# Sliding-window attention and a token MLP on one core: four stages in sequence, or one list-scheduled program

## The chip, the core and the metric

The kernel runs on one core of one Trainium2 chip. A core has five engines with queues of their own: TensorE (PE, matmuls, results only to PSUM), VectorE (DVE), ScalarE (ACT, activation functions), GpSimd (POOL) and SyncE (SP, which here only starts DMAs). Each engine works through its own instructions in the order in which the program gives them, and waits on semaphores for the others. PSUM is 8 banks of 128 x 512 float32. The metric is the device time of one execution in microseconds (us): 398.37 us, the median of three runs (398.35 to 398.4).

## The reference, cut to what matters

```python
def _A_ref(x, wqkv, wo):                      # x 1 x 2048 x 512, H = 32 heads of 16, window W = 256
    qkv = (x @ wqkv).reshape(B, S, 3, H, Dh).transpose(2, 0, 3, 1, 4)
    scores = jnp.einsum("bhqd,bhkd->bhqk", q, k) * (Dh ** -0.5)
    mask = (idx[:, None] - idx[None, :] >= 0) & (idx[:, None] - idx[None, :] < W)
    p = _softmax(jnp.where(mask, scores, -1e9))
    o = jnp.einsum("bhqk,bhkd->bhqd", p, v)
    return o.transpose(0, 2, 1, 3).reshape(B, S, D) @ wo
def _B_ref(x, w1, b1, w2, b2):                # mixes the 2048 tokens through F = 1376
    h = _layernorm(x)
    u = _gelu(jnp.einsum("bsd,sf->bdf", h, w1) + b1)
    return (jnp.einsum("bdf,fs->bds", u, w2) + b2).transpose(0, 2, 1)
g = _sigmoid((A_x * gate_w).sum(-1, keepdims=True))
return g * _A_ref(A_x, A_wqkv, A_wo) + (1 - g) * _B_ref(B_x...)
```

The kernel uses A_x for both branches, as the reference does. All tensors are bfloat16.

## The kernel before

Tokens are cut into 16 blocks of 128. The program is four stages, one after the other.

First the LayerNorm (L112 to L124: h_sb) and the gate (L126 to L136), from all of x (Xs, one load of 2 MB). x transposed (XT) comes from four transposing DMAs (L57). Then the first MLP matmul (L143 to L150): 11 chunks of F, each a chain of 16 matmuls of 128 x 512 into one PSUM bank, then GELU by hand on ACT and DVE (L153 to L161) into ug_sb. Third the projections (L192 to L213): Q twice, once with a copy of its weights in which the odd heads are zero (wqa) and once with the even ones zero (wqb), so that one 32-row operand (Qcomb) holds two heads side by side; K and V once; then the second MLP matmul (L215 to L225), 16 chains of 11, evacuated by ACT into b_sb.

Last the attention. A list of 180 steps (L243 to L248) runs over query block qb, the two or three key blocks kb that its window touches, and four groups gi of eight heads. emit_S does four score matmuls (L265: 32 rows by 256 columns, each for two heads, on two of the four 32-row groups of the array) into a two-bank PSUM tile Sp, one exp of 128 x 1024 on ACT (L273) into Et, and where the block is cut by the window a mask, on DVE (L275, diagonal) or POOL (L277, the far edge). Two steps later emit_PV does eight matmuls with Et as the loaded operand and 17 columns of V (16 and a column of ones, L301) into Op; after every second step DVE adds Op into osum in SBUF (L314, L316). When a query block is complete, emit_tailA normalises (L324, L326), transposes on PE (L333) and copies (L335); six steps later emit_tailB does the output projection (L342), the gated sum (L347, L349) and the store (L353). Sp has two buffers (ps_s), Et five (esb). The step list and the code order set the order on every engine.

Of the kernel before, what the change touches and what calls it, by code (L numbers as in the profile page):

```python
# [7 lines left out]
FP32 = mybir.dt.float32  # L9
# [4 lines left out]

@with_exitstack
def kernel(
# [21 lines left out]
    NQB = S // P  # L38
    NFC = (F + P - 1) // P
    EPS = 1e-5  # L40

# [3 lines left out]
    const = ctx.enter_context(tc.tile_pool(name="const", bufs=1))  # L45
    persist = ctx.enter_context(tc.tile_pool(name="persist", bufs=1))
    ugpool = ctx.enter_context(tc.tile_pool(name="ugpool", bufs=1))
    wts = ctx.enter_context(tc.tile_pool(name="wts", bufs=1))
    bphu = tc.alloc_tile_pool(name="bphu", bufs=1)

    Xs = persist.tile([P, NQB, D], BF16, name="Xs")
    nc.sync.dma_start(Xs[:], X.rearrange("(t p) d -> p t d", p=P))
    w1_sb = bphu.tile([P, NQB, F], BF16, name="w1_sb")
    nc.sync.dma_start(w1_sb[:], B_w1.rearrange("(t p) f -> p t f", p=P))
    XT = persist.tile([P, 4, S], BF16, name="XT")
    for ck in range(4):
# [12 lines left out]
    nc.gpsimd.dma_start(gw[:], gate_w.partition_broadcast(P))

    b1tmp = const.tile([P, NFC], BF16, name="b1tmp")
    b2tmp = const.tile([P, NQB], BF16, name="b2tmp")
    nc.gpsimd.memset(b1tmp[:], 0.0)
    with nc.allow_non_contiguous_dma(reason="tiny strided bias loads"):
        nc.gpsimd.dma_start(b1tmp[:, 0:NFC - 1], B_b1[0:(NFC - 1) * P].rearrange("(t p) -> p t", p=P))
        nc.gpsimd.dma_start(b1tmp[:F - (NFC - 1) * P, NFC - 1:NFC],
                            B_b1[(NFC - 1) * P:F].rearrange("(p o) -> p o", o=1))
        nc.gpsimd.dma_start(b2tmp[:], B_b2[:].rearrange("(t p) -> p t", p=P))

    ident = const.tile([P, P], BF16, name="ident")  # L80
# [156 lines left out]
    def e_col(kk, rl, par):  # L237
        return rl * 512 + kk * 256 + par * 128
# [164 lines left out]
```

## Time and profile before

| | us |
|---|---|
| median of three runs | 398.37 |
| span of the profiled execution, first to last instruction | 396.5 |
| MLP 1, projections, MLP 2 on PE | 32.8 to 170 |
| attention, 180 steps | 170.7 to 396.5 |
| PE busy / ACT busy / DVE busy / POOL busy | 340.3 / 229.1 / 203.4 / 81.2 |

No separate time is given for the profiled execution; its span is 1.9 us under the median, and that is taken as what lies around the span. To read the profile: a busy PE is not PE at its best, since matmuls overlap and their ends are modelled, so pitches (start to start) are used for PE; PEclk is the granted TensorE clock, 1.00 for 2.4 GHz and 0.50 for 1.2 GHz.

### The profile page before, as it was taken

How to read it: one execution, taken by the hardware profiler on the slowest of the kernel's cores; microseconds unless marked ns; L12 is line 12 of the kernel's file. 1: busy time of each engine (PE TensorE's matmuls, PEld its weight loads, DVE VectorE, ACT ScalarE, POOL GpSimd, SP SyncE). 2: the span in 40 equal slices, each digit the busy share in tenths (PEclk: the TensorE clock that was granted, in tenths of full speed). 3: DMA queues.
4: the chain of work that ended last, by engine and by line, in shares of the span. 5: the costliest groups of instructions: out<-in, count | busy, mean ns of one | idle time of the engine just before them, and what ended most of it. 6: DMA issues, size and time to landing. Idle time of an engine off the chain costs nothing.

```text
span 396.5 us, 6929 instructions
## 1 busy us (share of the span) xinstructions
PE 340.3 (86%) x2896; PEld 151.7 (38%) x2896; DVE 203.4 (51%) x410; ACT 229.1 (58%) x284; POOL 81.2 (20%) x80
## 2 busy tenths in 40 slices
PE   0006999899999999979999999999999999999982
PEld 0002444444444444433444444444344444444431
DVE  0199977743443100046556555545645645655653
ACT  1033433344333223277778778878877877977870
POOL 8300000020000000002143144044034124214300
PEclk9999999999999999985555555555555555555555
DMA  8999200096000000000000000000000000000000
GB/s 208 335 398 236 41 2 1 0 346 224 1 2 0 2 0 0 2 0 15 15 2 14 15 2 14 15 13 3 16 15 2 15 13 2 15 15 2 16 13 13
DMA packets 17423, 20.24 MB, mean 51 GB/s; under 512 B 8816, under 2 KB 13424, under 8 KB 17392
## 3 DMA queue, kind: packets, MB, share of 16 engines
q1 hardware_dynamic: 16160, 17.57, 13.7%
q10 hardware_dynamic: 1056, 2.10, 2.0%
q8 instruction: 22, 0.36, 0.4%
q0 software_dynamic: 176, 0.14, 0.3%
q14 instruction: 9, 0.07, 0.1%
HBM read 15.60 MB, written 2.10 MB: 45 GB/s over the span
## 4 chain that ended last, share of the span: by engine, by line
PE 46%; ACT 22%; DVE 13%; POOL 9%; DMA 4%; issue 4%; ACTq 0%; POOLq 0%
ACT Et L273 20%; PE Sp L265 10%; PE ps_proj L197 10%; PE ps_proj L219 10%; POOL Et L277 9%; PE aps L342 8%; PE Op L301 5%; DMA Xs<-in_A_x_dram 4%; PE ps_proj L208 3%; DVE stats L114 2%; DVE ug_sb L161 2%; DVE t L158 2%; DVE t L155 2%; ACT sg L160 2%; DVE h_sb L120 1%
## 5 line engine op out<-in xcount | busy, mean ns | idle before, releaser
L273 ACT ACTIVATE Et<-Sp 128x1024 bf16<-128x1024 f32 x180 | 173.3, 1028 | 42.1 <-PE Sp L265 42.0
L265 PE MATMUL Sp<-Qcomb,KT 32*128 32x256 bf16 x720 | 118.5, 393 | 8.7 <-ACT Et L273 7.9
L277 POOL TENSOR_SCALAR_AFFINE_SELECT Et<-Et 128x1024 bf16<-128x1024 bf16 x56 | 66.5, 1220 | 229.5 <-ACT Et L273 229.5
L301 PEld LDWEIGHTS <-Et 128*128 128x128 bf16 x1440 | 55.8, 106 | 89.5 <-DVE Et L275 38.8
L301 PE MATMUL Op<-VA,Et 128*128 128x17 bf16 x1440 | 69.8, 178 | 5.3 <-DVE Et L275 1.9
L148 PE MATMUL ups<-h_sb,w_sb 128*128 128x512 bf16 (+1 forms) x176 | 40.9, 397 | 33.3 <-DMA w_sb<-in_B_w_dram 32.8
L275 DVE TENSOR_TENSOR Et<-Et,Mge 128x1024 bf16<-128x1024 bf16 x64 | 42.8, 688 | 47.5 <-ACT Et L273 45.8
L316 DVE TENSOR_TENSOR osum<-Op,osum 128x272 f32<-128x272 f32 x58 | 25.6, 442 | 29.9 <-PE Op L301 29.9
L148 PEld LDWEIGHTS <-w_sb 128*128 128x128 bf16 (+1 forms) x176 | 18.2, 104 | 55.5 <-DMA w_sb<-in_B_w_dram 32.8
L219 PE MATMUL ps_proj<-ug_sb,w_sb 128*128 128x512 bf16 (+1 forms) x176 | 38.2, 379 | 0.0
L342 PE MATMUL aps<-wo_sb,OnT 128*128 128x512 bf16 x64 | 34.9, 610 | 0.5 <-DVE OnT L335 0.5
L265 PEld LDWEIGHTS <-KT 32*128 32x128 bf16 x720 | 26.9, 103 | 20.8 <-issue 16.6
L314 DVE COPY osum<-Op 128x272 f32<-128x272 f32 x32 | 14.1, 441 | 33.1 <-PE Op L301 32.0
L223 ACT ACTIVATE b_sb<-ps_proj,b2col 128x512 bf16<-128x512 f32 x16 | 11.0, 687 | 28.0 <-PE ps_proj L219 28.0
L219 PEld LDWEIGHTS <-w_sb 128*128 128x128 bf16 (+1 forms) x176 | 17.2, 98 | 20.9
L118 ACT ACTIVATE rstd<-mv,eps_col 128x1 f32<-128x1 f32 x16 | 4.6, 294 | 26.9 <-DVE mv L116 26.9
L183 ACT ACTIVATE Qcomb<-ps_proj 128x512 bf16<-128x512 f32 x16 | 11.8, 744 | 14.1 <-PE ps_proj L197 13.3
L185 DVE CAST Qcomb<-ps_proj 128x512 bf16<-128x512 f32 x16 | 11.6, 731 | 14.4 <-PE ps_proj L197 14.3
L160 ACT ACTIVATE sg<-t 128x512 f32<-128x512 f32 (+1 forms) x11 | 6.9, 630 | 20.5 <-DVE t L158 20.5
L197 PE MATMUL ps_proj<-XT,wqa 128*128 128x512 bf16 x64 | 14.1, 379 | 2.1 <-ACT uf L153 1.5
L347 DVE TENSOR_TENSOR diff<-aps,b_sb 128x512 f32<-128x512 f32 x16 | 11.1, 692 | 7.9 <-PE aps L342 7.9
L170 POOL MEMSET VA<- 128x512 bf16 x1 | 2.3, 2297 | 61.9 <-DVE ug_sb L161 61.9
(53 smaller groups left out, 231.4 us busy)
## 6 DMA issues: line engine op xcount, KB each, us to landing
w_sb<-in_B_w_dram SPq DMA_DIRECT2D x1, 5504.0 KB, 31.4
w_sb<-in_B_w_dram SPq DMA_DIRECT2D x1, 5120.0 KB, 17.1
Xs<-in_A_x_dram SPq DMA_DIRECT2D x1, 2048.0 KB, 17.7
out_dram<-outt SPq DMA_DIRECT2D x16, 128.0 KB, 1.7
wqkv_sb<-in_A_wqkv_dram ACTq DMA_DIRECT2D x1, 1536.0 KB, 13.5
wo_sb<-in_A_wo_dram ACTq DMA_DIRECT2D x1, 512.0 KB, 16.0
w_sb<-in_B_w_dram SPq DMA_DIRECT2D x1, 384.0 KB, 17.6
gw<-in_gate_w_dram POOLq DMA_DIRECT2D x1, 128.0 KB, 6.9
```

The costliest lines, as they stand in the source:

```text
L148: nc.tensor.matmul(ups[:fsz, :], lhsT=w1_sb[:, st, f0:f0 + fsz], rhs=h_sb[:, st, :], start=(st == 0), stop=(st == NQB - 1),)
L160: nc.scalar.activation(sg[:fsz, :], t1[:fsz, :], ACT.Tanh, scale=0.7978845608028654)
L197: nc.tensor.matmul(ps[:, :], lhsT=lhsT, rhs=XT[:, ck, sc * 512:(sc + 1) * 512], start=(ck == 0), stop=(ck == 3),)
L219: nc.tensor.matmul(yps[:, :], lhsT=w2_sb[:fsz, fc, st * P:(st + 1) * P], rhs=ug_sb[:fsz, fc, :], start=(fc == 0), stop=(fc == NFC - 1),)
L265: nc.tensor.matmul(Sp[:, col:col + 256], lhsT=KT[32 * r2:32 * r2 + 32, k, kb * P:(kb + 1) * P], rhs=rhs, start=True, stop=True, tile_posit ...
L273: nc.scalar.activation(out=Et[:], in_=Sp[:], func=ACT.Exp, scale=SCALE)
L275: nc.vector.tensor_tensor(out=Et[:], in0=Et[:], in1=Mge[:], op=ALU.mult)
L277: nc.gpsimd.affine_select(out=Et[:], in_=Et[:], pattern=[[0, 8], [-1, 128]], compare_op=ALU.is_gt, fill=0.0, base=0, channel_multiplier=1,)
L301: nc.tensor.matmul(Op[:, hl * DV:(hl + 1) * DV], lhsT=Et[:, col:col + 128], rhs=VA[:, kb, h, :], start=True, stop=True,)
L314: nc.vector.tensor_copy(out=dst, in_=Op[:, 0:16 * DV])
L316: nc.vector.tensor_tensor(out=dst, in0=Op[:, 0:16 * DV], in1=dst, op=ALU.add)
L342: nc.tensor.matmul(aps[:, :], lhsT=OnT[:, c2, :], rhs=wo_sb[:, c2, :], start=(c2 == 0), stop=(c2 == 3),)
```

## The change

The whole computation becomes a list of tasks (class Task: engines with a cost each, an emitting function, predecessors, a priority, buffers taken and used), and a planner (arrange) orders them once, when the program is built: it repeatedly takes the task that can start earliest by its costs, within a patience of 0.2 for the urgent ones by priority, gives it a buffer of a ring, and appends it. The instructions are then emitted in that order and stay in it on each engine.

- Attention goes by units of one query block, one half of the heads (hf, 16 heads) and one key block: 90 units. A unit is eight score matmuls on all four row groups into two Sp buffers (ring sp, three of two banks), two exps of 128 x 1024 into one Et of 128 x 2048 (ring et, five), one mask on 2048 columns, and 16 PV matmuls. The two or three key blocks of a group sum in one PSUM bank, so the adds of L316 and osum go; reciprocal and scaling read PSUM.
- Every other matmul result goes through ring gp, two banks: the projections, both MLP matmuls (chain, cut in pieces of two matmuls that other tasks can come between), PV, transposes, output projection, gate.
- Q is projected once; two evacuations multiply it by a 0/1 column (par) into QZ, one with the odd and one with the even heads zero. wqa and wqb go.
- x is loaded in four quarters, and XT comes from 64 PE transposes, evacuated by DVE. The gate's dot product goes to PE (64 matmuls of one column).
- The rstd is a power on POOL, and the tanh, exp and copies share one activation table. w1 and w2 share one buffer (wb), so w2's loads wait for the last MLP 1 matmul.
- Eight matmuls on zeros stand at the start of PE (warm). MLP 2 of a block is evacuated with gate and bias folded in (c1, c2), and one DVE instruction forms the output.

```diff
+def arrange(tasks, patience):
...
+            first = min(s for s, _ in found)
+            pick = min(
+                ((t.prio, s, i) for i, (s, t) in enumerate(found) if s <= first + (patience if t.prio < 10 else 0.0)),
+            )
+            start, t = found[pick[2]]
+            if best is None or (start, t.prio) < best[:2]:
+                best = (start, t.prio, e, t)
...
+    sp = ring("sp", 3, [P, 1024], FP32, "psum")
+    gp = ring("gp", 2, [P, 512], FP32, "psum")
+    et = ring("et", 5, [P, 2048], BF16, "sb")
...
-            nc.scalar.activation(rstd[:], mv[:, 1:2], ACT.Sqrt, bias=eps_col[:], scale=1.0)
+            nc.gpsimd.tensor_tensor(out=r, in0=r, in1=half[:], op=ALU.pow)
...
+    def chain(name, mms, deps, prio, piece=2):
+
+        b = gp.use()
...
+                    nc.tensor.matmul(buf(b)[:rows, :], lhsT=lhsT, rhs=rhs, start=(j == 0), stop=(j == n - 1))
...
+                for p in range(2):
+                    q.append(copy_out(
+                        f"qc{k}_{i}{p}", lambda k=k, p=p: QZ[:, i % NQ, p, k, :], lambda b=b: buf(b)[:],
+                        [t, k4] + free_q.get((k, i - NQ), []), 4, b, 0.53, scale=par[:, p:p + 1],
+                    ))
...
+    groups = [(qb, hf) for hf in range(2) for qb in range(4)]
+    groups += [(qb, hf) for qb in range(4, NT) for hf in range(2)]
...
-        for (kk, rl) in ((0, 0), (0, 1), (1, 0), (1, 1)):
+                for kk in range(2):
+                    k = 2 * hf + kk
+                    for r in range(4):
+                        nc.tensor.matmul(
+                            buf(b2[r // 2])[:, (r % 2) * 512 + kk * 256:(r % 2) * 512 + kk * 256 + 256],
...
+                            start=True, stop=True, tile_position=(32 * r, 0),
...
-                        lhsT=Et[:, col:col + 128],
-                        rhs=VA[:, kb, h, :],
-                        start=True, stop=True,
+                                buf(o)[:, hl * DV:(hl + 1) * DV], lhsT=buf(e)[:, col:col + 128], rhs=VA[:, kb, head, :],
+                                start=(first and hl == 0), stop=final, skip_group_check=True,
...
-                nc.vector.tensor_tensor(out=dst, in0=Op[:, 0:16 * DV], in1=dst, op=ALU.add)
...
+        dw2.append(add(f"w2_{i}", {"SP": 0.1}, emit, m1, 0.1 * i, lat=2.2 + 4.5 * (i + 1)))
...
+            lambda bp=bp, b=b, qb=qb: nc.scalar.activation(buf(bp)[:], buf(b)[:], ACT.Identity, bias=c2[:, qb:qb + 1], scale=c1[:, qb:qb + 1]),
...
+    plan = arrange(tasks, 0.2)
+    with tc.manual_schedule():
+        for t in plan:
+            t.emit()
```

What this does to the order shows at three places. **ACT in the attention.** Before, all 180 exps (L273) stand in one row behind everything else that ACT does:

```order
L183 ACTIVATE Qcomb<-ps_proj 128x512 x16
L183 ACTIVATE KT<-ps_proj 128x512 x8
L183 ACTIVATE VA<-ps_proj 128x32x16 x8
L223 ACTIVATE b_sb<-ps_proj,b2col 128x512 x16
L273 ACTIVATE Et<-Sp 128x1024 x180
```

Now (L474 is the exp, L637 the evacuation of an MLP 2 block into bp), around query block 8:

```order
L637 ACTIVATE bp_111<-gp_92,c_87,c_86 128x512
L474 ACTIVATE et_96<-sp_90 128x1024
L474 ACTIVATE et_96<-sp_88 128x1024
L474 ACTIVATE et_97<-sp_89 128x1024
L637 ACTIVATE bp_112<-gp_91,c_87,c_86 128x512
L474 ACTIVATE et_97<-sp_90 128x1024
L474 ACTIVATE et_93<-sp_88 128x1024
```

The evacuations stand between exps: the first exp comes after four evacuations instead of 102 activations of other kinds, and 65 other activations stand between the first exp and the last.

**PE in a late query block.** Before, PE alternates between four scores (L265) and eight PV matmuls (L301); only the output projection (L342) has 512 columns:

```order
L301 LDWEIGHTS Et
L301 MATMUL Op<-VA,Et 128x17
L265 LDWEIGHTS KT
L265 MATMUL Sp<-Qcomb,KT 128x256
L265 LDWEIGHTS KT
L265 MATMUL Sp<-Qcomb,KT 128x256
L265 LDWEIGHTS KT
L265 MATMUL Sp<-Qcomb,KT 128x256
L265 LDWEIGHTS KT
L265 MATMUL Sp<-Qcomb,KT 128x256
L342 LDWEIGHTS OnT
L342 MATMUL aps<-wo_sb,OnT 128x512
```

Now scores (L457) are followed by MLP 2 matmuls (L356, from ug and wb), here after the last unit's scores:

```order
L457 LDWEIGHTS KT
L457 MATMUL sp_90<-QZ,KT 128x256
L457 LDWEIGHTS KT
L457 MATMUL sp_90<-QZ,KT 128x256
L356 LDWEIGHTS wb
L356 MATMUL gp_92<-ug,wb 128x512
L356 LDWEIGHTS wb
L356 MATMUL gp_92<-ug,wb 128x512
L356 LDWEIGHTS wb
L356 MATMUL gp_92<-ug,wb 128x512
```

Between the first and the last score matmul PE now has 517 matmuls of 512 columns; before it had 60 there, all of the output projection.

**PE at the end.** Before, four output projection matmuls (L342) end the program:

```order
L333 LDWEIGHTS onrm
L333 MATMUL OnTp<-ident,onrm 128x128
L342 LDWEIGHTS OnT
L342 MATMUL aps<-wo_sb,OnT 128x512
L342 LDWEIGHTS OnT
L342 MATMUL aps<-wo_sb,OnT 128x512
```

Now the last MLP 2 chain (from ug and wb) and the last output projection (from wo and xo) do:

```order
L356 LDWEIGHTS wb
L356 MATMUL gp_92<-ug,wb 128x512
L356 LDWEIGHTS xo
L356 MATMUL gp_91<-wo,xo 128x512
L356 LDWEIGHTS xo
L356 MATMUL gp_91<-wo,xo 128x512
```

Behind the last score matmul stand 75 matmuls of 512 columns, 48 of PV and 4 transposes; before there were 24 of PV, 4 transposes and 4 of 512 columns.

## Rows read from the trace of the kernel before

**Rows 1.** The page: engine totals; then 40 slices, tenths busy and tenths of clock.
```profile
PE 340.3 (86%) x2896; PEld 151.7 (38%) x2896; DVE 203.4 (51%) x410; ACT 229.1 (58%) x284; POOL 81.2 (20%) x80
...
PE   0006999899999999979999999999999999999982
...
PEclk9999999999999999985555555555555555555555
```
**Rows 2.** The page: chain of work that ended last, shares of the span by engine.
```profile
PE 46%; ACT 22%; DVE 13%; POOL 9%; DMA 4%; issue 4%; ACTq 0%; POOLq 0%
```
**Rows 3.** Stretches: length; busy PE, PEld, DVE, ACT, POOL (x instructions); clock, DMA, GB/s.
```profile
79.90:118.00 38.10, 38.06 (x177) 17.28 (x177) 15.68 (x22) 15.78 (x23) 1.57 (x1) 1.00 0.40 149
132.00:170.00 38.00, 37.95 (x176) 17.03 (x175) 0.63 (x1) 10.32 (x16) 0.00 (x0) 1.00 0.00 1
171.00:175.00 4.00, 2.08 (x40) 1.01 (x33) 2.28 (x4) 3.78 (x5) 0.00 (x0) 0.96 0.00 0
175.00:385.00 210.00, 199.82 (x2224) 88.42 (x2223) 120.43 (x223) 168.50 (x175) 66.50 (x56) 0.50 0.03 11
```
**Rows 4.** Timeline of PE, high clock: start, length, line, operation, count, idle before.
```profile
170.73 0.41 PE L265 MATMUL Sp<-Qcomb,KT 32*128 32x256 bf16 x8 [0.78 <-ACT b_sb L223]
...
173.08 0.36 PE L301 MATMUL Op<-VA,Et 128*128 128x17 bf16 x8 [0.39 <-DVE Et L275]
173.37 0.40 PE L265 MATMUL Sp<-Qcomb,KT 32*128 32x256 bf16 x4
```
**Rows 5.** The same timeline of PE at the low clock.
```profile
176.98 0.61 PE L265 MATMUL Sp<-Qcomb,KT 32*128 32x256 bf16 x4
177.52 0.39 PE L301 MATMUL Op<-VA,Et 128*128 128x17 bf16 x8
177.84 0.61 PE L333 MATMUL OnTp<-ident,onrm 128*128 128x128 bf16 x4
178.38 0.61 PE L265 MATMUL Sp<-Qcomb,KT 32*128 32x256 bf16 x4
...
180.45 1.44 PE L342 MATMUL aps<-wo_sb,OnT 128*128 128x512 bf16 x3
181.82 0.61 PE L265 MATMUL Sp<-Qcomb,KT 32*128 32x256 bf16 x5
```
**Rows 6.** Timeline of ACT: exps that follow one another without a wait.
```profile
308.03 4.69 ACT L273 ACTIVATE Et<-Sp 128x1024 bf16<-128x1024 f32 x5 [1.12 <-PE Sp L265]
```
**Rows 7.** Groups by line and shape: busy us, mean ns | idle before, releaser.
```profile
L273 ACT ACTIVATE Et<-Sp 128x1024 bf16<-128x1024 f32 x180 | 173.3, 1028 | 42.1 <-PE Sp L265 42.0
...
L277 POOL TENSOR_SCALAR_AFFINE_SELECT Et<-Et 128x1024 bf16<-128x1024 bf16 x56 | 66.5, 1220 | 229.5 <-ACT Et L273 229.5
...
L183 ACT ACTIVATE Qcomb<-ps_proj 128x512 bf16<-128x512 f32 x16 | 11.8, 744 | 14.1 <-PE ps_proj L197 13.3 <-DVE ug_sb L161 0.8
...
L223 ACT ACTIVATE b_sb<-ps_proj,b2col 128x512 bf16<-128x512 f32 x16 | 11.0, 687 | 28.0 <-PE ps_proj L219 28.0
...
L153 ACT ACTIVATE uf<-ups,b1col 128x512 f32<-128x512 f32 x10 | 6.7, 673 | 0.2 <-DVE ug_sb L161 0.2
L160 ACT ACTIVATE sg<-t 128x512 f32<-128x512 f32 x10 | 6.3, 630 | 18.5 <-DVE t L158 18.5
...
L183 ACT ACTIVATE KT<-ps_proj 128x512 bf16<-128x512 f32 x8 | 4.8, 597 | 8.9 <-PE ps_proj L197 8.9
```
**Rows 8.** DMA issues: size and us from issue to landing.
```profile
w_sb<-in_B_w_dram SPq DMA_DIRECT2D x1, 5120.0 KB, 17.1
Xs<-in_A_x_dram SPq DMA_DIRECT2D x1, 2048.0 KB, 17.7
...
wqkv_sb<-in_A_wqkv_dram ACTq DMA_DIRECT2D x1, 1536.0 KB, 13.5
```
**Rows 9.** MLP 1 matmuls: count, shortest, median and longest ns, first and last start.
```profile
L148 PE MATMUL ups<-h_sb,w_sb x176: 376/379/634, 32.8 to 73.8; 128*128 128x512 bf16 x160, 128*96 128x512 bf16 x16
```
**Rows 10.** Timeline of the end: the last issue of a store.
```profile
393.46 0.33 SPq L353 DMA_DIRECT2D out_dram<-outt  x1
```

More of the change, by code (lines that the diff above doesn't have):

```diff
@@ L12, with __init__, use @@
 ALU = mybir.AluOpType
+class Buf:
+    def __init__(self, ring):
+        self.ring = ring
+        self.index = None
+        self.users = 0
+        self.end = 0.0
+class Ring:
+    def __init__(self, name, tiles):
+        self.name = name
+        self.tiles = tiles
+        self.avail = [0.0] * len(tiles)
+    def use(self):
+        return Buf(self)
+class Task:
+    def __init__(self, name, engines, emit, deps=(), prio=50.0, lat=None, takes=(), uses=(), at=0.0):
+        self.name = name
+        self.engines = dict(engines)
+        self.emit = emit
+        self.deps = [d for d in deps if d is not None]
+        self.prio = prio
+        self.lat = lat
+        self.takes = list(takes)
+        self.uses = list(uses)
+        for b in self.takes + self.uses:
+            b.users += 1
+        self.at = at
+        self.done = None
+        self.left = 0
+        self.next = []
+        self.ready = at
@@ new lines @@
+    KT = sb.tile([P, NK, 4, SB], BF16, name="KT")
+    QZ = sb.tile([P, NQ, 2, 4, SB], BF16, name="QZ")
+    VA = sb.tile([P, NT, H, DV], BF16, name="VA")
+    eps = sb.tile([P, 4], FP32, name="eps")
+    half = sb.tile([P, 4], FP32, name="half")
+    zeros = sb.tile([P, D], BF16, name="zeros")
+    ident = sb.tile([P, P], BF16, name="ident")
+    mask = sb.tile([P, P], BF16, name="mask")
+    par = sb.tile([P, 2], FP32, name="par")
+    gwc = sb.tile([P, 4], BF16, name="gwc")
+    b1t = sb.tile([P, NFC], BF16, name="b1t")
@@ new lines, in masks, with parity @@
+    def masks():
+        nc.gpsimd.memset(b1t[:], 0.0)
+        nc.gpsimd.memset(mask[:], 1.0)
+        nc.gpsimd.affine_select(
+            out=mask[:], in_=mask[:], pattern=[[1, P]], compare_op=ALU.is_ge, fill=0.0, base=0,
+            channel_multiplier=-1,
+        )
+    k2 = add("masks", {"POOL": 0.8}, masks, prio=1)
+    k3 = add("smalls", {"POOL": 4.0}, small_loads, [k2], prio=2, lat=6.0)
+    def parity():
+        v = ident[:].rearrange("p (r two d) -> p two r d", two=2, d=DH)
+        for i in range(2):
+            nc.vector.tensor_reduce(out=par[:, i:i + 1], in_=v[:, i], op=ALU.add, axis=mybir.AxisListType.XY)
@@ new lines, with biases @@
+    k4 = add("parity", {"DVE": 0.4}, parity, [k1], prio=0.5)
+    k5 = add("ones", {"POOL": 2.3}, lambda: nc.gpsimd.memset(VA[:, :, :, DH:DV], 1.0), prio=3)
+    def biases():
+        nc.vector.tensor_copy(b1c[:], b1t[:])
+        nc.vector.tensor_copy(b2c[:], b2t[:])
+    k6 = add("biases", {"DVE": 0.35}, biases, [k3], prio=30)
+    wu = gp.use()
+    warm = add(
+        "warm", {"PE": 3.4},
+        lambda: [nc.tensor.matmul(buf(wu)[:], lhsT=zeros[:, 0:P], rhs=zeros[:], start=True, stop=True) for _ in range(8)],
+        [k0], prio=0, takes=[wu],
+    )
```

707 lines of the change are left out of this document (428 added, 279 removed).

## Prediction

> **What bounds the kernel now.** First the page. PE is busy for 86% of the span, ACT for 58%, DVE for 51% [rows 1], and in the slices one sees that this is a mean over two programs: after the first loads PE is full all the way, but the TensorE clock is whole in the left half and half in the right. The chain that ended last gives PE 46% and ACT 22% [rows 2]. So the share of each engine has to be read by stage, and the stretches do that [rows 3]. In the projections PE is busy 38.06 of 38.10 us at clock 1.00, in MLP 2 37.95 of 38.00 us for 176 matmuls, a pitch of 38.0 / 176 = 0.216 us; ACT works 15.8 and 10.3 us there. These stages, from 32.8 to 170 us, have one limit, PE, and ACT's exps wait behind them. From 175 to 385 us PE is busy 199.8 of 210 us and ACT 168.5 of 210, and the clock is 0.50, which is 1.2 GHz. It fell some 5 us after the last 512-column matmul: from 171 to 175 us, with PE busy 2.08 of 4.00 us, it still averages 0.96. In the attention, then, PE at half clock is the limit and ACT is close behind: 180 exps need 173.3 us by their busy time [rows 7].
>
> The two halves use different engines, and nothing in the data forbids doing them together: MLP 1, MLP 2 and attention depend on each other only in the final sum. That is the room: 137 us of PE alone in front of 226 us of ACT and PE.
>
> **The change part by part: ACT.** An exp costs 4.69 / 5 = 0.938 us where five follow one another [rows 6]; 180 of them 168.8 us. Between the first and the last exp stand 65 others: 15 evacuations at 0.597, 16 that multiply by a column at 0.597 to 0.744 (I take 0.67), 11 bias adds at 0.673, 11 tanh at 0.630, 11 of MLP 2 at 0.687 [rows 7] and the gate's one of 0.2: 9.0 + 10.7 + 7.4 + 6.9 + 7.6 + 0.2 = 41.8 us. An exp alone takes 1.028 us against a pitch of 0.938, so neighbours overlap by 0.09, and 65 x 0.09 = 5.9 may come off: 205 to 211 us, and I take 207.
>
> **PE between first and last score.** At the high clock, dense matmuls: 517 x 0.216 = 111.7. Scores: a row shows eight of them, on all four row groups, within 0.41 us [rows 4], so a unit's eight cost at most 0.41; I take 0.40. PV: eight take 0.29 us from their start to the start of the next scores at the high clock [rows 4], 0.32 at the low one [rows 5]; sixteen 0.58. So 90 x 0.40 + 87 x 0.58 = 86.5. Transposes: four take 0.54 us at the low clock [rows 5], 0.135 each, and no more than that at the high one; 84 x 0.10 = 8.4. The gate's 64 columns go at the PV pitch of 0.036: 2.3. Sum 208.9. Removed with no cost left: 64 of the 128 Q matmuls (13.8 us at 0.216), and DVE's adds of PV.
>
> So ACT (207) and PE (209) are level over the same stretch, where before the same work stood at 137 + 214 us. Two engines that are both full and feed each other in a fixed order do not reach their sums. The row to size that by is the attention before: PE's needs per query block there are 12 x (0.54 + 0.32) + 0.54 + 4 x 0.43 = 12.6 us by pitch [rows 5], against 14.4 us that a block took (210 us for about 14.6 blocks), so 13% went into waits. Now there are three score buffers for two and room for ten exps for five, and I allow 6%: 12 us. Its ends are 0 and 13%, 27 us.
>
> **Start.** Before, all of wqkv (1.5 MB) landed after 13.5 us [rows 8]. The first score now needs two thirds of it: 9.0, from an issue at about 0.8: 9.8 us. A quarter of x is a quarter of 17.7 us, 4.4, and its transposes run before the weights are there. The bounds are 8 us (x quarter, 16 transposes and a copy alone set it) and 14.3 (the second load on the queue shares equally). Then four chains, 16 matmuls, at 0.216 or 0.432: after an idle stretch the first matmuls of MLP 1 took up to 634 ns against a median of 379 [rows 9], so PE begins low in spite of the eight on zeros; I take the middle, 5.2. An evacuation of 0.7 more: first score at 16, range 12 to 22. No sqrt table and no transposing DMA stand in the way any more; they cost the start nothing that is seen.
>
> **End.** Behind the last scores PE has 75 x 0.216 + 3 x 0.58 + 0.4 = 18.3 us of work; then one DVE instruction of 0.7 and the store, 396.5 - 393.46 = 3.0 us from its issue to the end [rows 10]: 22.0. The last exp ends some 2.3 us after the last scores, so 19.7 of it lie behind ACT. This is the price of two banks for all but scores: MLP 2 is not done when the exps are.
>
> **Covered.** w2 is loaded only after MLP 1's last matmul, since both weights share a buffer: 17.1 us for 5 MB [rows 8]. In the order eight units lie between that matmul and the first of MLP 2, 16 exps and some evacuations, 15 + 3 us, so it is hidden but for about 2 us, which the allowance holds; without that cover it would cost 17. POOL's masks double in size and halve in number, 28 x 2 x 1.22 = 68 us [rows 7] of 255. The power on POOL isn't in the trace: eight instructions of four columns, between nothing and 1.22 us each by the mask's row, needed first by MLP 1, fifty us later. DVE was busy 203 us in 396 [rows 1] and loses its adds into osum, so it has room, though its reciprocal and scaling now hold a PSUM bank.
>
> **Sum.** By ACT: 16.4 + 207 + 12 + 19.7 = 255. By PE: 16 + 209 + 12 + 22 = 259, with a score pitch that contains the end of the pipe. I take 255, and the 1.9 us that the median lies above the span: **257 us**.
>
> **The clock** carries this. All PE terms use the high level. The rows say that it is not idling alone that brings the low one: it was 0.50 with PE busy 95% [rows 3], on scores of 32 rows and PV of 17 columns. Where 512-column matmuls on 128 rows filled PE it was 1.00. In the new order the latter are 112 of the 209 us of PE's middle part, between the two; no row shows such a mixture. The Trainium skill, on the page "TensorE: Matmul & The Clock Gate", section "A second HAM failure mode: psum-queue depth-cycling", says that a kernel of 512-column matmuls which cycles through PSUM banks can idle so often between its groups that the clock swings between its levels. The trace before has no such swing in its projections over four banks, at 1.00 throughout [rows 3]; two banks are not in it. By that rule the time would be that of the third case below.
>
> **Rivals.** (1) *The two banks of gp.* 149 results go through them: chains, PV sums, transposes, output projections. A bank comes free after an evacuation of 0.6 to 0.74 us that may stand behind an exp of 0.94. If half of the takes hold PE for 0.5 us, that is 37 us in place of the 12: 257 + 25 = 282. For it: PE runs in one order and can't overtake. Against: the projections before lost 0.04 us in 38 with four banks. (2) *The clock falls in part.* Say it is low for the last 34 units, where only 165 dense matmuls stand: 165 x 0.216 + 34 x (0.14 + 0.06) = 42, so about 300; half of that 278, more stretches up to 345. (3) *The clock stays low throughout*: 608 dense matmuls cost 131 more, scores 90 x 0.14 = 13, PV 5, transposes some 9: 257 + 158 = 415, slower than now, and 464 if eight scores at the low clock take twice 0.54. It decides from about 90% of the work at the low level. Against it: a PE that falls behind at the low clock has its queue full of dense matmuls, which is what the rows show at the high one. (4) *Better than summed*: no stalls, start at 12, gives 238 or less.
>
> **How the numbers follow.** Forecast, 238 to 275: 0.62. (1) 275 to 305: 0.15. (2) 275 to 345: 0.14. (3) over 400: 0.05. (4) under 238: 0.04. The range of 238 to 305 holds the first, the second and half of the third, 0.84. A measurement of this kernel can tell about 0.2%. Faster by more than that: 0.95; within it 0.01; slower 0.04, of case (3).
>
> **What would show it.** Right: exps on ACT from about 17 us to 235 with hardly a gap, PEclk at 10 tenths in nearly all slices, PE busy over 85%, a last stretch of about 20 us in which ACT is nearly idle. Wrong: PE's waits for ACT or DVE to free gp summing to over 25 us (1); slices of PEclk at 5, and dense pitches of 0.43 us (2, 3); the first exp after 22 us (start); MLP 2's first matmul waiting for w2's DMA by over 5 us.

## The result, and the profile after

The changed kernel takes 272.25 us, the median of five runs (271.79 to 274.25), against 398.40 us of the kernel before beside it (398.35 to 398.44): a ratio of 0.6844, 95% interval 0.6824 to 0.6864. The prediction was 257 us with a range of 238 to 305. The profiled execution took 274.25 us itself, span 272.2; the other four have spans of 269.7 to 270.8. Below, the span is held against the predicted span of 255, and 2 us of the difference belong to this one execution.

The page first: engine totals; then 40 slices of the span, in tenths busy and tenths of the clock; then shares of the chain that ended last. It answers to [rows 1, 2].

```profile
PE 239.9 (88%) x2968; PEld 118.4 (43%) x2968; DVE 145.8 (54%) x256; ACT 214.2 (79%) x255; POOL 68.5 (25%) x50
...
PE   5588888888989999998798989899998989899894
...
DVE  0679977785566554758524574525425253443222
ACT  0239969689988977999569899999999999997221
...
PEclk9689979799997999999989999999999999999999
...
PE 56%; ACT 20%; DVE 15%; issue 4%; DMA 4%; DVEq 0%; ACTq 0%
```

The picture is the one that was forecast: the clock is whole in nearly every slice, PE and ACT are both near full from the fourth slice to the 36th, and in the last three ACT has nearly nothing to do. Two things in it were not forecast. PE shows 8 tenths about as often as 9, and ACT 5 to 8 in ten of these slices; and DVE, of which I had said that it has room, is at 7 to 9 tenths from the third slice to the ninth.

The stretches (length; busy PE, PEld, DVE, ACT, POOL with their instructions; clock, DMA share, GB/s): first exp to the end of the last one, then from there to the end, then two parts of the middle. They answer to [rows 3].

```profile
20.17:250.11 229.94, 209.73 (x2777) 104.72 (x2777) 131.58 (x225) 206.51 (x245) 59.95 (x34) 0.97 0.14 51
...
250.11:272.20 22.09, 17.11 (x121) 7.89 (x118) 4.67 (x8) 3.82 (x5) 0.23 (x1) 0.99 0.10 34
20.00:180.00 160.00, 144.30 (x1818) 70.90 (x1814) 101.69 (x176) 138.57 (x170) 38.13 (x23) 0.96 0.17 65
180.00:250.00 70.00, 65.49 (x964) 33.86 (x964) 30.07 (x49) 67.84 (x76) 21.71 (x11) 1.00 0.06 21
```

The sum had three parts, and each can be read off here: the first exp at 20.2 us (forecast 16.4), 229.9 us to the end of the last (219), 22.1 us behind it (19.7). So +3.8, +10.9 and +2.4. Inside the middle ACT is busy for 206.5 us, where 207 was forecast: the work was counted right, and the idle time of ACT is 23.4 us in place of the 12 allowed. Nearly all of it, 21.4 us, lies before 180 us; from there on ACT is busy 67.84 of 70 us.

Who ACT waits for between the first exp and the end of the last (engine, line, waited for: us in total, times, longest), where before the exps alone waited 42 us for scores [rows 7]:

```profile
ACT QZ L313 <- DVE QZ L317: 5.1, 5, 1.7
ACT uf L589 <- PE gp L356: 4.2, 5, 1.3
ACT et L474 <- PE sp L457: 2.7, 6, 1.2
...
ACT QZ L313 <- PE gp L356: 2.5, 3, 2.0
...
ACT bp L637 <- PE gp L356: 1.4, 6, 0.2
```

An exp hardly ever waits for its scores (2.7 us in 180 exps, 1.2 of them ahead of the first). Some 19 of the 23 us are waits of the evacuations and of MLP 1's steps that stand between the exps: in a fixed order an evacuation whose matmuls are not done holds up every exp behind it. The longest entry has DVE as its releaser: the two evacuations of one Q. The bp line waits another 14.7 us, but these lie in the last 22, behind the exps.

### The profile page after: what moved, and what is told of

It is laid out like the page before. It is cut to its first block, busy times and chain, and to the rows that moved or that the text cites. A ratio compares the mean times of both kernels' runs of the same rounds, so it can differ in the third digit from the quotient of the medians.

```text
span 272.2 us, 6817 instructions
## 1 busy us (share of the span) xinstructions
PE 239.9 (88%) x2968; PEld 118.4 (43%) x2968; DVE 145.8 (54%) x256; ACT 214.2 (79%) x255; POOL 68.5 (25%) x50
## 4 chain that ended last, share of the span: by engine, by line
PE 56%; ACT 20%; DVE 15%; issue 4%; DMA 4%; DVEq 0%; ACTq 0%
PE gp L356 41%; ACT et L474 12%; PE sp L457 7%; PE gp L512 7%; DMA wqkv<-in_A_wqkv_dram 4%; DVE QZ L317 3%; DVE et L483 3%; ACT QZ L313 3%; ACT bp L637 2%; DVE h L423 2%; DVE on L534 2%; DVE ug L611 1%; ACT uf L589 1%; DVE rd L527 1%; PE gp L548 1%
## 5 line engine op out<-in xcount | busy, mean ns | idle before, releaser
L474 ACT ACTIVATE et<-sp 128x1024 bf16<-128x1024 f32 x180 | 171.6, 1045 | 4.2 <-PE sp L457 2.7
L492 POOL TENSOR_SCALAR_AFFINE_SELECT et<-et 128x2048 bf16<-128x2048 bf16 x28 | 56.6, 2021 | 151.7 <-ACT et L474 131.7
L512 PEld LDWEIGHTS <-et 128*128 128x128 bf16 x1440 | 46.1, 96 | 23.6 <-issue 14.2
L483 DVE TENSOR_TENSOR et<-et,mask 128x2048 bf16<-128x2048 bf16 x32 | 39.1, 1223 | 31.5 <-ACT et L474 31.2
L512 PE MATMUL gp<-VA,et 128*128 128x17 bf16 x1440 | 48.2, 171 | 4.2 <-DVE QZ L317 1.1
L356 PE MATMUL gp<-h,wb 128*128 128x512 bf16 (+1 forms) x176 | 47.6, 386 | 0.0
L356 PE MATMUL gp<-ug,wb 128*128 128x512 bf16 (+1 forms) x176 | 44.5, 379 | 2.7 <-DVE on L534 2.6
L356 PEld LDWEIGHTS <-wb 128*128 128x128 bf16 (+2 forms) x352 | 29.9, 98 | 35.2 <-issue 10.9
L356 PE MATMUL gp<-XT,wqkv 128*128 128x512 bf16 x128 | 38.1, 420 | 8.1 <-DMA wqkv<-in_A_wqkv_dram 2.3
L457 PE MATMUL sp<-QZ,KT 32*128 32x256 bf16 x720 | 41.3, 277 | 3.5 <-ACT et L474 1.3
L457 PEld LDWEIGHTS <-KT 32*128 32x128 bf16 x720 | 13.3, 92 | 37.1 <-issue 35.8
L637 ACT ACTIVATE bp<-gp,c,c 128x512 f32<-128x512 f32 x16 | 12.4, 779 | 16.5 <-PE gp L356 16.1
L356 PE MATMUL gp<-wqkv,XT 128*128 128x512 bf16 x64 | 19.3, 407 | 3.8 <-ACT QZ L313 2.5
L527 DVE RECIPROCAL rd<-gp 128x16 f32<-128x16 f32 x32 | 8.1, 254 | 26.0 <-PE gp L512 15.2
L356 PEld LDWEIGHTS <-wqkv 128*128 128x128 bf16 x128 | 11.9, 103 | 22.8 <-issue 13.0
L356 PE MATMUL gp<-wo,xo 128*128 128x512 bf16 x64 | 17.7, 377 | 1.8 <-ACT bp L637 1.0
L317 DVE TENSOR_SCALAR QZ<-gp,par 128x512 bf16<-128x512 f32 x14 | 10.5, 750 | 15.2 <-ACT QZ L313 8.8
L406 DVE BATCH_NORM_STATS2 stats<-xo 128x6 f32<-128x512 bf16 x16 | 10.4, 681 | 5.5 <-DMA xo<-in_A_x_dram 5.5
```

Of the source, the lines that this page charges most:

```text
L317: nc.vector.tensor_scalar(out=out_(), in0=in_(), scalar1=scale, scalar2=None, op0=ALU.mult)
L356: nc.tensor.matmul(buf(b)[:rows, :], lhsT=lhsT, rhs=rhs, start=(j == 0), stop=(j == n - 1))
L457: nc.tensor.matmul(buf(b2[r // 2])[:, (r % 2) * 512 + kk * 256:(r % 2) * 512 + kk * 256 + 256], lhsT=KT[32 * r:32 * r + 32, (kb // 4) % NK ...
L474: lambda j=j, b2=b2, e=e: nc.scalar.activation(out=buf(e)[:, j * 1024:(j + 1) * 1024], in_=buf(b2[j])[:], func=ACT.Exp, scale=SCALE),
L483: lambda e=e: nc.vector.tensor_tensor(out=buf(e)[:].rearrange("p (n q) -> p n q", q=P), in0=buf(e)[:].rearrange("p (n q) -> p n q", q=P), ...
L492: lambda e=e: nc.gpsimd.affine_select(out=buf(e)[:], in_=buf(e)[:], pattern=[[0, 16], [-1, P]], compare_op=ALU.is_gt, fill=0.0, base=0, ch ...
```

## Experiments

All edits are to the changed kernel, and every kernel is planned anew by arrange, unless said otherwise. Times are medians, ratios to the kernel before on the same chip.

**How much is overlap, and how much the new form of the parts?** The MLP's first chains are made to depend on all normalisations, so that attention runs first and both MLPs behind it:

```diff
+            late = free_k.get((k, i - NK), []) if kind == "k" else free_q.get((k, i - NQ), [])
+            b, t = chain(f"{kind}{k}_{i}", mms, [dwk, xt[i, 0], xt[i, 1], warm] + late, prio)
...
+        nms.append(nm)
...
+        b, t = chain(f"u{fc}", mms, dw1 + hready + nms, 22 + fc)
```

> The changed program with one dependency more: MLP 1 starts only after the last attention group is normalised, so the attention runs alone and both MLP matmuls stand behind it; all other parts (PSUM sum, one Q projection, quarter loads, ring sizes) stay. Theory A, the gain is mostly overlap: attention then needs its ACT time without the MLP's (about 185 us plus stalls, from 20 us on), and behind it MLP 1 38 us, w2's load 17, MLP 2 and output projection 52, end 5: 320 to 335 us, so overlap is worth 50 to 60 of the 126 us gained and the clock falls to 0.50 once the projections are over. Theory B, the gain is mostly the clock: at 0.50 the attention becomes bound by PE and takes over 210 us, and the time goes to 350 or more. Theory C, the cheaper parts alone did it: under 300 us.

Measured: 328.65 us (327.91 to 329.39), ratio 0.8248 [0.8225, 0.8271]. Its stretches, columns as above:

```profile
100.00:140.00 40.00, 32.65 (x530) 17.33 (x533) 18.20 (x29) 38.84 (x45) 12.03 (x6) 0.73 0.01 2
140.00:180.00 40.00, 33.57 (x528) 16.06 (x523) 15.20 (x28) 40.00 (x45) 14.77 (x8) 0.50 0.01 2
180.00:220.00 40.00, 32.78 (x502) 16.50 (x503) 13.28 (x24) 34.03 (x38) 13.29 (x7) 0.50 0.01 2
220.00:260.00 40.00, 36.72 (x165) 16.65 (x166) 21.45 (x33) 14.49 (x22) 0.00 (x0) 0.99 0.11 41
```

Of the 126 us gained, 328.65 - 272.25 = 56 come from doing the MLP under the attention, and 70 from the rest, in which the projections already lie between the exps. The part that I had not seen: alone, without dense matmuls, the clock falls to 0.50 as before, and yet ACT is busy 40.00 of 40.00 us with PE at 33.6. Where PE was the limit of the attention before (199.8 of 210 us busy, [rows 3]), ACT is now, even at 1.2 GHz; which of the new parts does that (eight scores on four row groups, more score buffers, another order) was not tested apart. The exps run from 19.9 to 213.7 us, 194 us with the projections between them, where before they took 215 without.

**The two banks of gp**, the first rival: a buffer of two banks is taken from the scores and given to everything else.

```diff
+    sp = ring("sp", 2, [P, 1024], FP32, "psum")
+    gp = ring("gp", 4, [P, 512], FP32, "psum")
```

> PSUM cut otherwise: four banks for everything but scores (two before), two score buffers (three before); the planner orders anew. Theory A, the 21 us that ACT stands idle between 20 and 180 us come from the two banks: idle falls by half or more, 258 to 264 us. Theory B, the score buffers matter more than the banks: exps wait for scores, 275 to 290 us. Theory C, neither: within 2 us of 272.

Measured: 306.45 us (304.81 to 306.75), ratio 0.7683, 34 us slower and worse than either theory said. The page's exps and scores (busy, mean ns | idle before, releaser):

```profile
PEclk9999999995899999999699999999985555555555
...
L474 ACT ACTIVATE et<-sp 128x1024 bf16<-128x1024 f32 x180 | 176.8, 1021 | 44.5 <-PE sp L457 43.9
...
L457 PE MATMUL sp<-QZ,KT 32*128 32x256 bf16 x720 | 54.4, 312 | 30.7 <-ACT et L474 29.1
```

With two score buffers each unit's scores wait for the exps of the unit before: 29.1 us on PE, 43.9 on ACT. The dense matmuls, which now have banks enough, run ahead and are used up (the last one of MLP 2 starts at 222.7 us), and from there the clock is at 0.5. So in this exchange the third score buffer is worth more than two banks of gp. What two more banks would be worth by themselves it does not tell, since both were changed at once.

**ACT's own load**: all evacuations of Q, K and V on DVE.

```diff
+  both=False        # in the three copy_out calls of Q, K and V
```

> All evacuations of Q, K and V go to DVE (34 stood on ACT). Theory A, ACT's fixed order is what stalls: an evacuation that is not ready holds up exps behind it, so without them the time falls by the 10 to 20 us of their own work and waits, to 255 to 264 us. Theory B, DVE's queue becomes the holder of the banks: 272 to 280 us.

Measured: 271.05 us (270.17 to 271.33), ratio 0.6795 [0.6782, 0.6809]: 1.2 us less, beside both theories. ACT has 20 us less to do (194.3 against 214.2 busy). First exp to the end of the last, and from there to the end, columns as above:

```profile
20.32:235.52 215.20, 193.12 (x2691) 100.24 (x2732) 146.07 (x256) 186.83 (x211) 60.27 (x34) 0.98 0.14 53
235.52:269.60 34.08, 27.86 (x163) 12.23 (x163) 6.92 (x11) 6.19 (x9) 0.28 (x1) 0.99 0.10 34
```

The exps do run through sooner, in 215.2 us for 229.9. But PE then has more left behind them (117 matmuls of 512 columns behind the last score in place of 75), and the last stretch grows from 22.1 to 34.1 us. What ACT is spared is lost again there, where PE works off what is left nearly alone. On the way DVE is busy 43.55 of the 45 us from 20 to 65.

**Which engine sets the pace?** Two kernels add work in the order of the changed kernel without moving a thing: 90 copies of 128x128 on ACT, one behind every second exp; and 92 of the MLP's matmuls issued a second time, 44 in MLP 1 and 48 in MLP 2 (their products are then summed twice, which changes the MLP's values); what was expected of it counts 81 of them, some 2.4 us too few.

```diff
+                    ), nc.scalar.activation(junk[:], zeros[:, 0:P], ACT.Copy) if j else None),
```

> The changed program in the same order on every engine, with one small copy of 128 x 128 more on ACT behind every second exp (90 of some 0.2 us, about 18 us of ACT, writing a tile that nothing reads). Theory A, ACT sets the pace of the attention's length: 15 to 18 us longer, 287 to 290. Theory B, PE does: under 5 us longer, since ACT has 24 us of idle between first and last exp. Theory C, neither alone, they wait for each other in turn: 6 to 14 us.

```diff
+                    more = name[0] in "uy" and j % 4 == 1
+                    if more:
+                        nc.tensor.matmul(buf(b)[:rows, :], lhsT=lhsT, rhs=rhs, start=False, stop=(j == n - 1))
```

> The changed program in the same order, with every fourth matmul of both MLP chains done twice (81 of 0.216 us, 17.5 us of PE; the repeated products are added again, so the MLP branch has other values). Some 13.5 of them stand before the last score's matmul, 4 behind it. Theory A, ACT sets the pace and PE has room: the 4 us behind the last score and little else, 274 to 278. Theory B, PE sets it: 15 to 18 us longer, 287 to 290. Theory C, in turn: 8 to 14 us.

Measured: ACT's copies add 14.9 us to its busy time and 6.2 us to the whole (278.48, 277.63 to 279.33); PE's matmuls add 16.0 us of busy time and 15.75 us (288.0, 287.7 to 288.3). The first and last start of MLP 2's matmuls (durations min/median/max ns, then the starts), in the changed kernel, then with ACT's copies, then with the doubled matmuls:

```profile
L356 PE MATMUL gp<-ug,wb x176: 376/379/389, 176.1 to 267.5; 128*128 128x512 bf16 x160, 96*128 96x512 bf16 x16
...
L357 PE MATMUL gp<-ug,wb x176: 376/379/390, 178.5 to 272.7; 128*128 128x512 bf16 x160, 96*128 96x512 bf16 x16
...
L357 PE MATMUL gp<-ug,wb x176: 376/379/389, 181.0 to 281.6; 128*128 128x512 bf16 x160, 96*128 96x512 bf16 x16
```

MLP 1's 44 extra ones, 9.5 us at 0.216, push MLP 2's start by 4.9; the 48 in MLP 2, 10.4 us, push its end by 9.2 more. So of PE's additions half arrive before 176 us and nearly nine tenths behind it; of ACT's four tenths in all, 2.4 us at MLP 2's start and 2.8 more at its end. These are single profiles, of a kernel whose spans differ by 2.5 us from run to run. With the experiment before, in which 20 us less of ACT gave 1.2, it follows that the time goes by PE's work more than by ACT's, most of all behind 176 us, though not by PE's alone.

**The planner's costs.** Ten costs are set to what the trace of the changed kernel shows (scores 0.40 to 0.34, PV 0.44 to 0.41, exp 0.96 to 0.94, DVE mask 1.15 to 1.23, POOL mask 2.3 to 2.0, transposes 0.3 to 0.4, gate 1.8 to 3.0, and three others). Then, on top of that, the planner is told that the second evacuation of a Q can't start before the first has ended:

```diff
-                        [t, k4] + free_q.get((k, i - NQ), []), 4, b, 0.53, scale=par[:, p:p + 1],
+                        [t, k4] + q[:1] + free_q.get((k, i - NQ), []), 4, b, 0.53, scale=par[:, p:p + 1],
```

> Only the planner's costs change, to what the trace shows: eight scores 0.34 for 0.40, sixteen PV 0.41 for 0.44, exp 0.94 for 0.96, MLP 2's evacuation 0.70 for 0.72, tanh 0.60 for 0.55, the DVE mask 1.23 for 1.15, POOL's 2.0 for 2.3, four transposes 0.40 for 0.30, DVE copies 0.06 more, the gate's matmuls 3.0 for 1.8. Theory A, the stalls come from an order made with wrong costs: 3 to 8 us less, 264 to 269. Theory B, a fixed order loses that much whatever the costs, since waits are not foreseen to a tenth of a us: within 3 us of 272.

> The corrected costs of the run before, and the planner told that the two evacuations of one Q result follow each other (the trace shows that two engines never read one bank at the same time there, 15 us of waits in all; the planner took them as parallel). Theory A, an order that is made with what really waits loses less: 3 to 6 us below the run with corrected costs, 263 to 266. Theory B, noise of the planner: within 2 us of 269, or worse.

Measured: 269.13 us (269.1 to 270.18), ratio 0.6761 [0.6748, 0.6774], with the costs, which is where its two theories meet; 264.58 us (263.46 to 265.13), ratio 0.6637 [0.6621, 0.6654], with both. The work is the same; the order differs, and with it which of ACT and DVE does some evacuations: 3.1 and then 4.6 us more. ACT's waits with both, over the whole span:

```profile
ACT bp L637 <- PE gp L356: 19.5, 8, 5.7
...
ACT QZ L313 <- DVE QZ L317: 1.0, 1, 1.0
```

The wait of one Q evacuation for the other, 6.2 us over the whole span of the changed kernel, falls to 1.0 on ACT, ahead of the first exp, and from 8.8 to 0.3 on DVE. From first exp to the end of the last, then from 20 to 180 us, where ACT is now busy for 148.0 us (138.6 in the changed kernel) and PE for 150.3 (144.3):

```profile
20.47:236.30 215.83, 203.83 (x2749) 101.35 (x2749) 130.68 (x220) 203.24 (x242) 60.94 (x34) 0.98 0.14 53
20.00:180.00 160.00, 150.31 (x1977) 74.14 (x1976) 106.44 (x181) 148.00 (x181) 42.90 (x25) 0.98 0.17 65
```

ACT's idle time among the exps falls from 23.4 to 12.6 us, about as much as the forecast of the middle had missed, and PE's idle time there from 20.2 to 12.0. Not all of it arrives at the end: the stretch behind the last exp grows from 22.1 to 26.3 us, since more of MLP 2 is left by then. But each is one order. How far another small change of the costs would move the time by chance was not measured, so that it is these corrections, and not a luckier order, is shown only for the waits of one Q evacuation for the other, 5.1 us of the 23.4.

**DVE's load at the start**: the 16 scalings of h on POOL.

```diff
-                f"h{t_}", {"DVE": 0.4},
-                lambda t_=t_: nc.vector.tensor_scalar(
+                f"h{t_}", {"POOL": 1.0},
+                lambda t_=t_: nc.gpsimd.tensor_scalar(
```

> The LayerNorm's 16 scalings (h) go from DVE to POOL. In the first 60 us DVE is busy 18.6 and 15.7 of 20 us, and one scaling that stands beside a POOL mask took 2.09 us for 0.40. Theory A, DVE and this contention hold up the first 60 us: 3 to 8 us less, 264 to 269. Theory B, POOL is too slow for it and MLP 1 waits for h: 275 or more. Theory C, the order's fixed place of MLP 1 keeps the time: within 2 us of 272.

Measured: 270.63 us (269.85 to 271.55), 1.6 us less, little more than the spread of the runs. One takes a median of 2.07 us on POOL against 0.40 on DVE; DVE is 7.7 us less busy, and that moves little.

**The start.** One kernel without seven of the eight matmuls on zeros, and, on top of the better order (264.58 us), one that lets the weights of Q and K and the first quarter of x land before the other loads begin, one that fills PE's idle time ahead of the projections with 14 more matmuls on zeros (six at the start, eight behind the first transposes), and one with both.

```diff
-        ... for _ in range(8)],
+        ... for _ in range(1)],
```

> The changed program with one of the eight matmuls on zeros at PE's start instead of eight. Theory A, they do nothing for the projections, since PE stands idle from 8.4 to 10.7 us and the first twelve projection matmuls run at a pitch of 0.43 us as it is: within 1 us of 272. Theory B, they raise the clock for what follows: 1.5 to 4 us longer.

```diff
+        dx.append(load(f"x{i}", emit, 512, deps=[dwk], prio=0.1 * i, small=2.2 + 1.6 * i))
...
+        dw1.append(load(f"w1_{i}", emit, 1376, deps=[dwk], prio=1 + 0.1 * i, small=12.6 + 4.2 * i))
```

> As the run with corrected costs and serial Q evacuations (264.6 us), and the loads of x's later quarters, V's weights, w1 and wo are issued only when the Q and K weights have landed. Theory A, the first 1.5 MB then land at about 7 us instead of 10.6, and PE, which sets the pace, starts that much earlier: 2 to 4 us less, 260 to 263. Theory B, the later loads come as much too late, MLP 1 or the second quarter waits: 264 or more.

```diff
+                if i == 0 and c == 1:
+                    for n_ in range(8):
+                        nc.tensor.matmul(sp.tiles[0][:, 0:512], lhsT=zeros[:, 0:P], rhs=zeros[:], start=True, stop=True)
```

> As the run of 264.6 us, with fourteen instead of eight matmuls on zeros at PE's start and eight more behind the first sixteen transposes, so that PE hardly idles before the weights land. Theory A, the first projections then run at 0.216 us instead of 0.43: 12 x 0.21 = 2.5 us less, about 262. Theory B, the evacuations behind them set the start: within 1 us. Theory C, the zeros themselves run long and delay the projections: 265 to 267.

> The corrected costs and the serial Q evacuations of e11, with both edits of the start together: weights first as in e12 and the zero matmuls of e13. Each of the two alone brought the first exp from 20.5 to 18.4 us and the time down by 1.5 us. Theory A (they shorten different things, the landing and the projections' pitch, so they add): first exp before 17.3 us, 261 to 262.3 us. Theory B (both stop at the same next thing, the evacuations and the two banks behind the first chains): first exp at 18 us or later, 262.4 to 263.4 us. Bounds for the time: under 261 or over 263.4 neither.

Measured: without the zeros 271.2 us (270.41 to 272.03), ratio 0.6806 [0.6787, 0.6824], no worse than with them. Weights first 263.02 (262.59 to 263.45), the fill 263.06 (262.42 to 264.3), both together 260.88 (260.83 to 262.62), ratio 0.6567 [0.6549, 0.6585]. PE at the start, first the changed kernel (start, length, line, operation, count, idle before):

```profile
7.27 1.07 PE L334 MATMUL gp<-ident,xo 128*128 128x128 bf16 x16 [2.42 <-DMA xo<-in_A_x_dram]
10.65 5.30 PE L356 MATMUL gp<-XT,wqkv 128*128 128x512 bf16 x12 [2.31 <-DMA wqkv<-in_A_wqkv_dram]
15.80 0.61 PE L334 MATMUL gp<-ident,xo 128*128 128x128 bf16 x8
16.63 0.61 PE L334 MATMUL gp<-ident,xo 128*128 128x128 bf16 x8 [0.22 <-ACT KT L311]
17.26 1.02 PE L356 MATMUL gp<-XT,wqkv 128*128 128x512 bf16 x4
18.12 0.61 PE L334 MATMUL gp<-ident,xo 128*128 128x128 bf16 x8
18.66 0.29 PE L457 MATMUL sp<-QZ,KT 32*128 32x256 bf16 x4
19.85 0.29 PE L457 MATMUL sp<-QZ,KT 32*128 32x256 bf16 x4 [0.90 <-DVE QZ L317]
```

and with both edits:

```profile
7.72 1.07 PE L334 MATMUL gp<-ident,xo 128*128 128x128 bf16 x16 [1.53 <-DMA xo<-in_A_x_dram]
8.62 1.89 PE L342 MATMUL sp<-zeros 128*128 128x512 bf16 x8
10.54 1.90 PE L361 MATMUL gp<-XT,wqkv 128*128 128x512 bf16 x8
12.70 0.81 PE L361 MATMUL gp<-XT,wqkv 128*128 128x512 bf16 x3 [0.25 <-ACT KT L311]
14.01 0.59 PE L361 MATMUL gp<-XT,wqkv 128*128 128x512 bf16 x2 [0.50 <-ACT QZ L313]
```

In the changed kernel the first twelve projection matmuls go at 0.43 us each, half clock, behind an idle PE (2.31 us); with matmuls right up to them, at 0.216. The eight on zeros at the very start are followed by transposes and idle time, and without seven of them the time is the same. The weights' edit did not work as expected: the weights were to land at about 7 us, but their load took 9.2 us with the others held back, where it took 9.3 to 9.8 in four kernels with them. What comes sooner are the last four projections, which start at 15.2 in place of 17.2 us: 16 transposes of x's later quarters, which now land later, no longer all stand before them. The first exp starts at 20.5 us in the better order, 18.4 with either edit and 17.2 with both, so at the start the two add up in part. In the time it is -1.5 each and -3.7 together, with intervals of about 1 us. The time lies 0.1 us under the stretch that theory A gave, outside of what was named for either theory. This is the fastest kernel of the study, 11.4 us under the changed one.

## Why the prediction was right, and where its terms were off

**What bounds the kernel: held.** Attention and the MLPs overlap, the clock stays up, and PE and ACT are both near full. The first experiment prices the overlap at 56 us. I had looked for the gain in the room of 137 us of PE; the other 70 us come from elsewhere, as the rows suggest without a test of each: a first score at 18.7 us where PE began its first matmul at 32.8, 64 matmuls fewer, the projections among the exps, and an attention that ACT, not PE, limits even at the low clock. Not held is that ACT and PE count alike: I took the sum by ACT, and added or removed work shows that the time goes by PE more than by ACT (15.75 us for the doubled matmuls, 6.2 for ACT's copies, 1.2 for 20 us less of ACT).

**ACT: held.** 206.5 us against 207. One row was too cheap: the evacuation of MLP 2 with two operands by column takes a mean of 779 ns, where b_sb with one took 687 [rows 7].

**PE: the sum looks right and is not.** PE shows 208.68 us busy from the first score to the last, and 208.9 was the sum; that they agree is luck. Busy counts the end of each matmul's pipe. By pitches in the late, full part of the timeline (start, length, line, operation, count):

```profile
245.12 0.59 PE L356 MATMUL gp<-wo,xo 128*128 128x512 bf16 x2
245.64 0.40 PE L457 MATMUL sp<-QZ,KT 32*128 32x256 bf16 x8
245.97 0.56 PE L512 MATMUL gp<-VA,et 128*128 128x17 bf16 x16
246.39 0.59 PE L356 MATMUL gp<-wo,xo 128*128 128x512 bf16 x2
246.82 0.55 PE L512 MATMUL gp<-VA,et 128*128 128x17 bf16 x16
```

sixteen PV take 0.42 us, where I took 0.58: 87 x 0.16 = 14 us too much. Eight scores take 0.33 us for 0.40, but that is no gain, since what goes before scores pays for them: two 512-column matmuls take 0.52 us up to the next scores (245.12 to 245.64) and 0.43 up to PV (246.39 to 246.82). The PV price came from the distance between eight PV and the scores behind them [rows 4], doubled. At 0.42 / 16 = 0.026 us each eight PV are 0.21, so some 0.08 of the 0.29 was this step to scores, and the price held it twice. PE's need is then about 195 us, and the 14 us too much hid part of the next error.

**The allowance for two engines that feed each other: mis-sized.** 12 us allowed, 23 us measured, within the stated ends of 0 and 27. The cause is not the one that I sized it by (PE and ACT waiting for scores). Some 19 us of it are waits of the evacuations and MLP 1's steps in ACT's row, 5.1 of them for a Q evacuation on DVE that the order took to run beside ACT's; with the costs and that dependence put right, ACT's idle time between the first exp and the end of the last is 215.8 - 203.2 = 12.6 us. The timeline shows one such pair, DVE's first, from 14.28 us on, and ACT's:

```profile
14.28 0.75 DVE L317 TENSOR_SCALAR QZ<-gp,par 128x512 bf16<-128x512 f32 x1 [2.93 <-PE gp L356]
...
19.04 0.75 DVE L317 TENSOR_SCALAR QZ<-gp,par 128x512 bf16<-128x512 f32 x1 [0.36 <-ACT QZ L313]
```

```profile
15.07 0.69 ACT L313 ACTIVATE QZ<-gp,par 128x512 bf16<-128x512 f32 x1 [1.04 <-DVE QZ L317]
...
18.32 0.69 ACT L313 ACTIVATE QZ<-gp,par 128x512 bf16<-128x512 f32 x1 [1.74 <-PE gp L356]
```

ACT starts at 15.07, when DVE has ended (15.03), though both only read the same chain's bank; at 19.04 it is the other way round. It is not the common output tile that keeps them apart: two evacuations from different banks into VA, one on each engine, overlap by 0.26 us from 173.10 us on. The Trainium skill, page "PSUM — Partial Sum Buffer", section "PSUM bank collisions raise a hardware error", says that no two engines may touch one bank on the same partitions at a time, two readers included, and that a dependency has to keep them apart. The trace agrees, 15 us of such waits in all (6.2 on ACT, 8.8 on DVE), and this is the rule that I should have held against "two evacuations multiply it".

**The start: mis-sized**, 18.7 us in place of 16 for the first score. The weights landed at 10.6 us (9.8 forecast). Twelve matmuls at half clock took 5.2 us, where I had taken that for all sixteen, with the middle of the two levels. The rest is some 2 us of transposes of x's later quarters, which the order puts before the last four projections and before the first scores (15.80 to 17.26 and 18.12 to 18.66) and which the sum does not have.

**DVE "has room": wrong at the start.** The busy share of 54% is a mean; in the stretch from 20 to 40 us DVE is busy 18.6 of 20 us, more than PE (16.9) and ACT (17.4):

```profile
20.00:40.00 20.00, 16.89 (x219) 8.15 (x216) 18.62 (x38) 17.44 (x21) 3.21 (x3) 0.91 0.59 226
```

I read the bound of the kernel by stage and then judged DVE by the page's mean. What it cost in all is open; taking the h scalings off DVE gave 1.6 us.

**w2: held; POOL: by luck.** The first matmul of MLP 2 starts at 176.1 us without a wait for its weights. POOL is busy 68.5 us, but the 68 was for its masks alone, and these take 56.6 (28 of 2.02 us); the rest is other work, of which the powers (1.02 us each) delay nothing that is seen.

**The end: held nearly**, 22.1 us for 19.7. PE is busy 17.11 of those 22.09 us, the rest are short waits for evacuations; the last store adds its 3 us.

**Rivals.** (1) Two banks: in part. From the first exp's scores to the last scores PE waits some 16 us for evacuations out of gp, most of them to have a bank free; the sign that I had named was 25. The two longest entries:

```profile
PE gp L356 <- ACT QZ L313: 4.2, 5, 1.3
PE gp L356 <- DVE on L534: 3.7, 7, 0.7
```

For score buffers or Q it waits 3 us. So the rival had the place right, and its price of 37 us too high; the 272 us lie between the forecast and its 282. The second experiment does not refute it, since it took a score buffer for the banks. (2) The clock: in part. Behind the start it dips in four short spells, of which the timeline shows one:

```profile
84.32 1.01 PE L356 MATMUL gp<-h,wb 128*128 128x512 bf16 x2
85.26 0.61 PE L457 MATMUL sp<-QZ,KT 32*128 32x256 bf16 x8
...
87.53 0.59 PE L356 MATMUL gp<-h,wb 128*128 128x512 bf16 x2
```

Two 512-column matmuls take 0.94 us to the start of the next scores in it, and 0.52 at the high clock in the timeline above (from 245.12). Over five executions of the changed kernel the mean clock goes from 0.962 to 0.987 and the span from 272.2 to 269.7, so what the spells cost is some 2.5 us between the worst and the best, not the 18 to 88 of the rival. Swings that cost about 1% are thus there with two banks. The Trainium skill, page "TensorE: Matmul & The Clock Gate", section "A second HAM failure mode: psum-queue depth-cycling", has a kernel of 512-column matmuls swing between the clock's levels as it cycles through PSUM banks. That the two banks cause the swings here is not shown: in the second experiment, with four, the slices 10, 11 and 20 of PEclk are at 5, 8 and 6 while dense matmuls are still left. (3) Low throughout: wrong, mean clock 0.962. But the second experiment shows its mechanism: when MLP 2's matmuls were used up at 222.7 us, the clock was soon at 0.5, and stayed there to the end.

## What to carry to other kernels

When a program is ordered by a list of costs, what the list has wrong goes into the order: ten costs corrected, and one pair of operations that the planner took for parallel and the program runs in series, came with 7.7 us less for the same work, if by one order each. Ask which engine's work the time follows before relieving another: 20 us less of ACT gave 1.2 us. Judge every engine by stage, the ones with a low mean too, and take a pitch from rows in which nothing waits, up to the next matmul of another kind. Here the clock was at 0.50 with small matmuls alone and at 0.97 with dense ones mixed in, as long as these lasted.

## What the runs showed of the hardware

- Matmuls on zeros helped here only when they ran right up to the work: eight of them with idle time behind changed nothing (271.2 us without seven of them, 272.25 with), 14 more that filled PE's gaps brought the next eight projections from 0.43 to 0.216 us each.
- The load of 1 MB of weights took 9.3 to 9.8 us in four kernels with other loads beside it, and 9.2 and 9.7 in the two with most of them held back: the neighbours hardly set its time here.
- Two 512-column matmuls take 0.52 us up to the start of 32-row scores and 0.43 up to PV of 128 rows, both at the high clock.
- A scaling of h of 128x512 on DVE has a median of 0.40 us, but four that began at 57.89 us took 3.06 us together, one of them 2.09, while POOL ran a mask from 58.02 to 60.16. In the kernel before the longest was 0.41. That the two engines get in each other's way there was not tested apart.
- An ACT evacuation of 128x512 with two operands of one column each takes a mean of 779 ns, with one 687 [rows 7] and 692 (QZ).
- A POOL mask of twice the columns takes 2.02 us against 1.22 [rows 7], not twice; a POOL power of four columns takes 1.02 us.
